# Threshold attention followed by a squared-ReLU feed-forward layer: one weight tile with fourteen stores, x^T loads in four periods, a reordered head with more unread transposes, and another order of the PSUM pools

## The chip, the cores and the metric

The kernel runs on one NeuronCore of a Trainium2 chip. The core has five engines that run side by side and meet at semaphores: TensorE (PE; its weight loads are listed as PEld), VectorE (DVE), ScalarE (ACT), GpSimd (POOL) and SyncE (SP), which here does nothing but issue DMAs. The metric is device time in microseconds; less is better. All data is float32, apart from the two weight matrices, which arrive as 64-bit floats and are converted on the chip.

## The reference

```
q, k, v: (8, 8, 576, 64)            # batch, heads, sequence, head size
scores = q @ k^T / 8
scores = where(scores >= rowmax(scores) - 0.02, scores, -1e9)
attn   = softmax(scores)             # divided by (sum + 1e-9)
x      = (attn @ v), heads side by side   # (4608, 512)
h      = maximum(x @ w_in, 0)             # w_in  (512, 2048)
out    = (h * h) @ w_out                  # w_out (2048, 512)
```

## The kernel before

**Attention.** The 64 heads are handled as 32 pairs. Queries come in blocks of 128 (four full ones per pair, and the remaining 64 rows of two pairs together), which gives 144 units; a unit covers both heads of its pair. The Python loop calls `period(p)` for p = -2 to 74, and a period takes two units, `A = 2p` and `B_ = 2p + 1`, through the stages of a software pipeline: scores, softmax, the transposes of the softmax weights of an earlier period (`fill`, `filled`), the product with v (`values`), and the store of the result to DRAM (`give_x`, then `ask`). The order in a period is written out by hand, and the engines keep it: each runs its own instructions strictly in the order in which they stand.

What matters for the change:

- `load_q`, `load_k`, `load_v` bring a pair's q, k, v. `turn(i, 0)` and `turn(i, 1)` transpose q and k of pair `i` on TensorE (four 128x128 transposes into the PSUM tile `pqk`), and ScalarE copies them out (lines 353 and 350). `turn_last` does the last 64 rows of both (`pqkr` or `pL`), with ScalarE copies in lines 369 and 370 and a GpSimd copy into the block-diagonal tile `kdiag` (line 373).
- `scores(n)` makes the 512 main columns of a unit's scores (line 411), `scores_rest(n)` the last 64 (line 386, which needs `kdiag`), into a PSUM tile `sc` of three banks. There are two such tiles, so unit n + 2 waits until VectorE has read unit n.
- VectorE takes the row maximum (`top`, line 428), ScalarE the exponential (line 436), VectorE masks and sums (line 441), GpSimd normalizes (line 453).
- `filled` copies transposed weights to SBUF on ScalarE (line 505). Its target `wT` exists once, and the results that `ask` stores to the DRAM tensors `xT` lie in the front of the same tile. So the copy of the next period waits for these stores to land.
- [...] During attention the pool `sc_pool` has two tiles of three banks and `b_pool` two tiles of one bank, which all other users take in turn.

**Weights, beside the attention.** `fetch` loads a chunk of w_out or w_in (line 183), `convert1` to `convert6` make 32-bit floats of it, one chunk per period, in the order of the periods: `convert1` stands in ScalarE's queue (line 203) ahead of the copies that end a `turn`. From period 15 on `sums` (GpSimd, lines 132 and 135) forms the 49 blocks of w_out that the fast matrix product needs, one or more per period. Since the blocks of w_in take the same places, `keep(m)` puts the seven finished blocks of row m on a list, and `ask(False)`, called twice in every period, stores up to two of them to DRAM each time (line 565). Stores, loads of q, k and v, weight chunks and results all stand in SP's one queue, in the order in which the periods issue them.

**Feed-forward.** Both products use 7-product block multiplication twice (49 products where 64 would be plain). Tokens go in nine steps of 512. `hidden_layer` (matmuls `ph`, line 807) makes squared hidden values and stores them to DRAM; in its last step `reload` brings the 49 blocks of w_out back (line 1028). `output_layer` (matmuls `po`, line 942) makes the output. `load_x(n)` loads a step's x^T with four or six DMAs (line 740). For step 0 that happens in period 27, at `IN_FIRST - 6`, and from period 34 on each period forms one of its block sums on GpSimd. The PSUM pool `banks` is opened when the attention's pools are closed: six tiles for products, and two tiles `c` for operands that `sum_v` copies through PSUM.

**The head.** Before the first period the kernel issues the loads of pair 0, ten transposes of the identity matrix whose result nobody reads (`keep_busy(10)`, line 996), then `turn(0, 0)`, `turn(0, 1)` and `turn_last(0)`. `TURNS` says in which period a later `turn` happens; those of g = 2 and g = 3 (q and k of pair 1) are both in period 1.

Of the kernel before, what the change touches and what calls it, by code (L numbers as in the profile page):

```python
# [10 lines left out]
FP32 = mybir.dt.float32  # L11
# [37 lines left out]
def kernel(  # L49
# [25 lines left out]
    nc = tc.nc  # L75
    B, H, S, D = q.shape
    P = 128
# [7 lines left out]
    BANK = 512  # L85
# [4 lines left out]

    PSUM = bass.MemoryType.PSUM
    const = ctx.enter_context(tc.tile_pool(name="const", bufs=1))
    wp = ctx.enter_context(tc.tile_pool(name="wp", bufs=1))
    dram = ctx.enter_context(tc.tile_pool(name="dram", bufs=1, space=bass.MemoryType.DRAM))
    xT = [dram.tile([DM, S], FP32, name=f"xT{b}") for b in range(B)]
    gT = [[dram.tile([P, BANK], FP32, name=f"g{n}_{j}") for j in range(16)] for n in range(NSTEP)]
# [9 lines left out]
    ident = const.tile([P, P], FP32, name="ident")  # L106
# [4 lines left out]
        out=tau_c[:, :], in_=bass.AP(tensor=tau.tensor, offset=tau.offset, ap=[[0, P], [1, 1]])  # L111
# [28 lines left out]
    OUTER, INNER = (1, 2, 6, 7, 4, 5, 3), (1, 6, 2, 7, 5, 4, 3)  # L140
# [5 lines left out]


    W_IN, W_OUT = {}, {}

    def weight_tile(W, m, k):  # L150
        at = OUTER.index(m) * 7 + INNER.index(k)
        W[m, k] = wp.tile([P, BANK], FP32, tag=f"w{at}", name="w")
        return W[m, k]

    def blocks(at):
# [101 lines left out]

    def keep(m):

        for k_ in INNER:  # L260
            w_dram[m, k_] = dram.tile([P, BANK], FP32, name=f"w{m}{k_}")
            later.append((w_dram[m, k_][:, :], W_OUT[m, k_][:, :]))

    later = deque()

# [199 lines left out]
    TURNS = {}  # L465
    for g in range(2, 2 * len(pairs)):
        two, x = divmod(g - 4, 4)
        TURNS.setdefault(max(1, (9 * two + 5 + 2 * x) // 2), []).append(g)

    def turned_last(p):  # L470

# [72 lines left out]
    def has(n):  # L544
        return 0 <= n < NU
# [12 lines left out]
    def ask(every=True):  # L558

        while given:  # L560
            to, from_ = given.popleft()
            nc.sync.dma_start(out=to, in_=from_)
        for _ in range(len(later) if every else min(2, len(later))):
            to, from_ = later.popleft()
            nc.sync.dma_start(out=to, in_=from_)

# [9 lines left out]
    def period(p):  # L576

        A, B_, a, b = 2 * p, 2 * p + 1, 2 * p - 2, 2 * p - 1
        m, turns = p - 2, TURNS.get(p, ())
        sc = {}  # L580

        def first(f, pv):
            if has(2 * m) or has(2 * m + 2):
                pt = pv[f] if pv else bank([P, BANK], "pX")
                fill(m + 1, f, pt)
                return pt

        def other(m, f):
            if has(2 * m):
                pt = bank([P, BANK], "pY")  # L590
                fill(m, f, pt)
                return pt

        def begin(n):
            if has(n) or has(n - 4):
                sc[n] = sc_pool.tile([P, 3 * BANK], FP32, tag="sc", name="sc")
            if has(n):
                scores_rest(n, sc[n])

        def spare(m, f, n):  # L600
            if has(2 * m):
                pt = sc[n][:, SPARE : SPARE + 3 * P]
                fill(m, f, pt)
                return pt

        pt3 = other(m, 4)
        then = None
        if turned_last(p):
            at = pt3 if pt3 else bank([P, BANK], "pL")
            then = turn_last(turns[-1] // 2, at[:, 3 * P : 4 * P])  # L610
        begin(A)
        do(b, "mask", 0)
        convert3(begun(p - 1))
        do(b, "mask", 1)
        ptA = spare(m, 2, A)
        if has(A):
            scores(A, sc[A])
            softmax(A, sc[A])
        if pt3:
            filled(m, 4, pt3)  # L620
        if then:
            then()
        last = [turn(g // 2, g % 2) for g in turns]
        if ptA is not None:
            aside(A, filled(m, 2, ptA))
        convert1(begun(p))
        pt2 = other(m, 3)
        do(a, "inverse")
        do(b, "over")
        do(A, "top")  # L630
        convert4(begun(p - 1))
        begin(B_)
        ptB = spare(m, 5, B_)
        do(a, "normal", 1)
        for done in last:
            done()
        if pt2:
            filled(m, 3, pt2)
        do(A, "least")
        if ptB is not None:  # L640
            aside(B_, filled(m, 5, ptB))
        do(A, "power", 0)
        do(a, "normal", 0)
        if has(B_):
            scores(B_, sc[B_])
            softmax(B_, sc[B_])
        do(b, "inverse")
        do(B_, "top")
        do(A, "power", 1)
        do(A, "mask", 0)  # L650
        do(A, "mask", 1)
        convert2(begun(p))
        pv = values(m) if has(2 * m) else None
        do(b, "normal", 1)
        do(B_, "least")
        pt0 = first(0, pv)
        pt1 = first(1, pv)
        do(b, "normal", 0)
        do(B_, "power", 0)
        sums_step()  # L660
        if pt0:
            filled(m + 1, 0, pt0, pv)
        convert5(begun(p - 1))
        do(A, "over")
        do(B_, "power", 1)
        if pt1:
            filled(m + 1, 1, pt1, pv)
        if pv:
            valued(m)
            give_x(m, wT[m + 1], plans[m + 1].size[0])  # L670
        ask(False)
        convert6(begun(p - 1))
        if begun(p - 1) is None:
            sums_step()
        sums_start(p)
        if begun(p - 1) is None and not turned_last(p):
            sums_step()
        fetch(begun(p + 2))
        ask(False)
        for n in (A, B_):  # L680
            if has(n) and units[n][1] == FULL:
                for i in units[n][0]:
                    turned.pop(i)
# [41 lines left out]

    prepared = {}

    def load_x(n):
        at = X_AT[n % 2]
        xo = arena[:, ds(at, 7 * BANK)].rearrange("p (m c t) -> p m c t", m=7, c=2)  # L730
        for a, c in ((0, 0), (1, 0), (1, 1), (0, 1)):
            to = xo[:, AT_B[a][c] - 1, :, :]

            t0 = n * STEP + c * 2 * NQ
            done = 0
            while done < 2 * NQ:
                b, at = divmod(t0 + done, S)
                m = min(S - at, 2 * NQ - done)
                src = xT[b][ds(a * 2 * P, 2 * P), ds(at, m)].rearrange("(c p) n -> p c n", p=P)
                nc.sync.dma_start(out=to[:, :, ds(done, m)], in_=src)  # L740
                done += m
        prepared[n] = (xo, None)

    def sum_v(op, out, x, y):

        c = banks.tile([P, BANK], FP32, tag="c", bufs=2, name="c")
        n = 1
        for m in y.shape[1:]:  # L750
            n *= m
        c = c[:, 0:n].rearrange("p (a b) -> p a b", b=y.shape[2])
        nc.scalar.copy(c, y)  # L753
        return lambda: op(nc.vector, out, x, c)
# [227 lines left out]
            w()  # L982

    with tc.manual_schedule():
        with ExitStack() as stack:
            sc_pool = stack.enter_context(tc.tile_pool(name="sc", bufs=2, space=PSUM))
            b_pool = stack.enter_context(tc.tile_pool(name="b", bufs=2, space=PSUM))

            def bank(shape, name):
                return b_pool.tile(shape, FP32, tag="b", name=name)  # L990

            def keep_busy(times):

                pt = bank([P, P], "idle")
                for _ in range(times):
                    nc.tensor.transpose(pt[:, :], ident[:, :], ident[:, :])

            load_q(0)
            load_k(0)
            first = sb.tile([P, 4, 2], FP32, tag="small", bufs=4, name="small")  # L1000
            nc.scalar.activation(out=first[:, 0, :], in_=ident[:, 0:2], func=AF.Exp)
            load_v(0)
            keep_busy(10)
            turn(0, 0)()
            turn(0, 1)()
            turn_last(0, bank([P, P], "pqkr")[:, :])()
            for i in range(1, 3):
                load_v(i)
            xsums = iter(())
            for p in range(-2, NU // 2 + 3):  # L1010
                period(p)
                if p == IN_FIRST - 6:
                    load_x(0)
                    xsums = prepare_x(0, lambda op, out, x, y: op(nc.gpsimd, out, x, y))
                if p > IN_FIRST:
                    next(xsums, None)
            for _ in xsums:
                pass
            for _ in range(60):
                sums_step()  # L1020
            ask()
        banks = ctx.enter_context(tc.tile_pool(name="banks", bufs=1, space=PSUM))

        def reload(at):

            m, k = OUTER[at // 7], INNER[at % 7]
            t = weight_tile(W_OUT, m, k)
            nc.sync.dma_start(out=t[:, :], in_=w_dram[m, k][:, :])

        for n in range(NSTEP):  # L1030
            last = n == NSTEP - 1
# [103 lines left out]
```

## Time and profile before

| | us |
|---|---|
| median of 3 runs | 1383.01 |
| lowest and highest run | 1382.67, 1388.16 |
| the profiled execution | 1383.25 |
| its span on the engines | 1381.5 |
| TensorE busy | 1339.5 (97%) |
| VectorE, GpSimd, ScalarE busy | 1025.5, 990.1, 860.5 |
| DMA traffic | 177.24 MB |

In the rows of the timeline the first number is the start in us from the start of the span, the second the duration, then the engine, the line, the operation, and its tiles (output first) with shapes and count; brackets at the end give how long the engine was idle before it and what ended that. SPq is SP's issue of a DMA: its duration is that of the issue, and not of the transfer. In the tables by stage each pair of numbers is busy us and instructions of PE, PEld, DVE, ACT and POOL; the last three columns are the granted TensorE clock, the mean busy share of the DMA engines, and GB/s. The attention lasts to about 583 us of the span, the hidden layer to 981, the output layer to the end. A matmul of 128x128 float32 operands is two instructions in the trace.

### The profile page before, as it was taken

To read this page: it belongs to the slowest core of one execution; us is meant where nothing else is said; L and a number is where in the kernel's file an instruction comes from. 1 tells how busy PE (TensorE), PEld (TensorE's weight loads), DVE (VectorE), ACT (ScalarE), POOL (GpSimd) and SP (SyncE) were. 2 spreads that over 40 slices of the span, in tenths; PEclk is the share of its full clock that TensorE was granted. 3 is DMA by queue.
4 is the path that set the end of the run, shared out by engine and by line. 5 is a ranking of instruction groups with operands and counts; after the bars stand their busy time and mean duration, and the time that the engine had idled before them with its cause. 6 is when DMAs were issued, how large, how long until landed. Compare 5 with 4: busy or idle time off the path is not lost. (4 is left out here: it accounts for less than half of the span.)

```text
span 1381.5 us, 40859 instructions
## 1 busy us (share of the span) xinstructions
PE 1339.5 (97%) x15882; PEld 1180.6 (85%) x15882; DVE 1025.5 (74%) x2136; ACT 860.5 (62%) x1651; POOL 990.1 (72%) x1111
## 2 busy tenths in 40 slices
PE   7999999899999999999999999999999999999998
PEld 4676767666767676799999999999999999999998
DVE  5999988789998888577778777887666456654563
ACT  5999877789987777656766566765733224332330
POOL 2777888798888886355566556656877777777776
PEclk9999999999999999999999999999999999999999
DMA  4554325786532322123432343338962344224411
GB/s 115 128 150 127 92 63 149 222 260 192 139 89 67 73 65 57 36 83 129 146 128 87 108 146 130 108 106 325 370 223 64 120 154 153 93 71 144 153 32 31
DMA packets 205295, 177.24 MB, mean 128 GB/s; under 512 B 96304, under 2 KB 149552, under 8 KB 205104
## 3 DMA queue, kind: packets, MB, share of 16 engines
q1 hardware_dynamic: 203792, 174.24, 40.9%
q8 instruction: 125, 2.05, 0.6%
q14 instruction: 66, 0.54, 0.1%
q10 hardware_dynamic: 1312, 0.41, 0.1%
HBM read 105.12 MB, written 69.47 MB: 126 GB/s over the span
## 5 line engine op out<-in xcount | busy, mean ns | idle before, releaser
L135 POOL TENSOR_TENSOR arena<-arena 128x512 f32<-128x512 f32 (+1 forms) x314 | 376.4, 1221 | 250.1 <-DVE arena L135 210.4
L807 PE MATMUL ph<-arena,w 128*128 128x128 f32 x3528 | 396.6, 275 | 1.8 <-ACT arena L505 0.8
L807 PEld LDWEIGHTS ph<-arena,w 128*128 128x128 f32 x3528 | 394.7, 192 | 3.7 <-DVE arena L135 2.8
L942 PE MATMUL po<-w,arena 128*128 128x128 f32 x3528 | 396.6, 275 | 0.3
L942 PEld LDWEIGHTS po<-w,arena 128*128 128x128 f32 x3528 | 394.8, 192 | 1.9 <-issue 1.6
L135 DVE TENSOR_TENSOR arena<-ph,arena 128x512 f32<-128x512 f32 x378 | 255.3, 688 | 93.7 <-PE ph L807 62.4
L441 DVE SCALAR_TENSOR_TENSOR arena<-sc,arena 128x576 f32<-128x576 f32 x288 | 223.0, 811 | 16.4 <-ACT arena L436 16.0
L428 DVE TENSOR_REDUCE arena<-sc 128x2 f32<-128x1152 f32 x144 | 195.1, 1355 | 53.5 <-PE sc L411 49.2
L135 DVE TENSOR_TENSOR arena<-po,arena 128x128 f32<-128x128 f32 x378 | 107.8, 289 | 169.7 <-PE po L942 166.2
L436 ACT ACTIVATE arena<-sc,arena 128x576 f32<-128x576 f32 x288 | 207.2, 750 | 42.3 <-DVE arena L428 36.7
L453 POOL TENSOR_SCALAR arena<-arena 128x576 f32<-128x576 f32 x288 | 213.9, 757 | 19.0 <-DVE arena L450 11.2
L753 ACT COPY c<-arena 128x512 f32<-128x512 f32 (+1 forms) x303 | 172.8, 580 | 62.4 <-DVE arena L132 55.0
L516 PEld LDWEIGHTS pv<-arena 64*64 64x64 f32 x5760 | 151.6, 133 | 40.1 <-issue 21.7
L132 POOL TENSOR_TENSOR arena<-arena 128x512 f32<-128x512 f32 (+1 forms) x138 | 174.5, 1264 | 9.7
L132 DVE TENSOR_TENSOR arena<-arena,c 128x512 f32<-128x512 f32 (+1 forms) x267 | 174.5, 661 | 7.5 <-ACT c L753 6.5
L411 PE MATMUL sc<-arena 64*64 64x512 f32 x1152 | 159.5, 624 | 0.0
L516 PE MATMUL pv<-arena 64*64 64x128 f32 (+1 forms) x5760 | 157.9, 259 | 0.4 <-ACT arena L353 0.2
L786 ACT ACTIVATE arena<-arena 128x512 f32<-128x512 f32 x144 | 89.9, 624 | 76.9 <-POOL arena L135 76.7
L721 ACT COPY arena<-po 128x128 f32<-128x128 f32 x63 | 16.6, 264 | 179.2 <-PE po L942 177.4
L499 PE MATMUL pY<-ident,arena 128*128 128x128 f32 x546 | 85.9, 278 | 28.3 <-ACT arena L505 24.8
L447 POOL TENSOR_SCALAR arena<-arena 128x2 f32<-128x2 f32 x144 | 47.5, 330 | 83.9 <-DVE arena L441 46.1
L499 PEld LDWEIGHTS pY<-ident,arena 128*128 128x128 f32 x546 | 60.0, 140 | 51.9 <-issue 25.3
(63 smaller groups left out, 1247.6 us busy)
## 6 DMA issues: line engine op xcount, KB each, us to landing
g<-arena SPq DMA_DIRECT2D x144, 256.0 KB, 2.0
arena<-g SPq DMA_DIRECT2D x144, 256.0 KB, 4.6
w<-w SPq DMA_DIRECT2D x98, 256.0 KB, 5.1
arena<-in_v_dram SPq DMA_DIRECT2D x32, 288.0 KB, 3.1
out_dram<-arena SPq DMA_DIRECT2D x70, 128.0 KB, 2.2
arena<-in_q_dram SPq DMA_DIRECT2D x64, 128.0 KB, 3.2
arena<-in_moe_w_out_dram SPq DMA_DIRECT2D x16, 512.0 KB, 4.3
xT<-arena SPq DMA_DIRECT2D x128, 64.0 KB, 2.1
```

Of the source, the lines that this page charges most:

```text
L132: e.tensor_tensor(out=out, in0=x, in1=y, op=ALU.subtract)
L135: e.tensor_tensor(out=out, in0=x, in1=y, op=ALU.add)
L411: made = nc.tensor.matmul(sc[at, ds(j * 2 * BANK, MAIN)], lhs, kT[rows, 0:MAIN], start=True, stop=True)
L428: nc.vector.tensor_reduce(out=nmx, in_=both, axis=AXIS.X, op=ALU.max, negate=True)
L436: nc.scalar.activation(out=w[:, :, j, :], in_=of(j), func=AF.Exp, bias=nmx[:, j : j + 1], scale=1.0)
L441: nc.vector.scalar_tensor_tensor(out=w[:, :, j, :], in0=of(j), scalar=thr[:, j : j + 1], in1=w[:, :, j, :], op0=ALU.is_ge, op1=ALU.mult, a ...
L453: nc.gpsimd.tensor_scalar(out=w[:, :, j, :], in0=w[:, :, j, :], scalar1=rs[:, j : j + 1], scalar2=1.0, op0=ALU.mult, op1=ALU.mult)
L499: nc.tensor.transpose(to, w[:, c, :, :].rearrange("p j d -> p (j d)"), ident[:, :])
L516: nc.tensor.matmul(out[j][ds(u * D, D), ds(row, count)], loaded_v[i][rows, c, :], x[rows, ds(plans[m].at[u, c] + row, count)], start=(c == ...
L753: nc.scalar.copy(c, y)
L807: nc.tensor.matmul(to[:, j, :], W_IN[m, k][:, ts(j, P)], of[k][:, m - 1, :], start=(not more and j == 0), stop=True, skip_group_check=True,)
L942: nc.tensor.matmul(to, g[:, j, :], w[:, j, :], start=(not more and j == 0), stop=(j == 3), skip_group_check=True)
```

## The change

It has five parts.

1. The 49 separate weight tiles become slices of one tile `wall`. `keep(m)` makes one DRAM tensor of seven blocks per row m and lists two stores in place of seven, one of four blocks (128x2048) and one of three (128x1536): 14 stores in all. `ask(False)` sends at most one store, and its second call in a period is gone. `reload` reads slices of the new DRAM tensors.
2. The four loads of x^T for step 0 go out one per period, in periods 23 to 26.
3. The head has more unread TensorE work: 15 transposes in place of 10; between `turn(0, 0)` and `turn(0, 1)` eight 64-row transposes, two whole ones, sixteen 64x64 matmuls and two whole ones again; four after `turn_last(0)`; twenty after period 0.
4. In period 0 the main scores of unit 0 stand ahead of its last 64 columns, and the `turn` of pair 1's q moves from period 1 to period 0.
5. `b_pool` is opened first and stays open to the end; the feed-forward's pool `banks` then has the six product tiles alone, and `sum_v` takes its tiles from `b_pool`.

```diff
-        W[m, k] = wp.tile([P, BANK], FP32, tag=f"w{at}", name="w")
+        W[m, k] = wall[:, ds(at * BANK, BANK)]
...
-        for k_ in INNER:
-            w_dram[m, k_] = dram.tile([P, BANK], FP32, name=f"w{m}{k_}")
-            later.append((w_dram[m, k_][:, :], W_OUT[m, k_][:, :]))
+        to = dram.tile([P, 7 * BANK], FP32, name=f"w{m}")
+        for i, k_ in enumerate(INNER):
+            w_dram[m, k_] = to[:, ts(i, BANK)]
+        for i, z in ((0, 4), (4, 7)):
+            at = OUTER.index(m) * 7 + i
+            later.append((to[:, ds(i * BANK, (z - i) * BANK)], wall[:, ds(at * BANK, (z - i) * BANK)]))
...
-        TURNS.setdefault(max(1, (9 * two + 5 + 2 * x) // 2), []).append(g)
+        TURNS.setdefault(max(g - 2 if g < 4 else 1, (9 * two + 5 + 2 * x) // 2), []).append(g)
...
-        for _ in range(len(later) if every else min(2, len(later))):
+        for _ in range(len(later) if every else min(1, len(later))):
...
-            if has(n):
+            if n > 0 and has(n):
                 scores_rest(n, sc[n])
...
             scores(A, sc[A])
+            if A == 0:
+                scores_rest(A, sc[A])
             softmax(A, sc[A])
...
         fetch(begun(p + 2))
-        ask(False)
...
-        c = banks.tile([P, BANK], FP32, tag="c", bufs=2, name="c")
+        c = b_pool.tile([P, BANK], FP32, tag="b", name="c")
...
     with tc.manual_schedule():
+        b_pool = ctx.enter_context(tc.tile_pool(name="b", bufs=2, space=PSUM))
         with ExitStack() as stack:
             sc_pool = stack.enter_context(tc.tile_pool(name="sc", bufs=2, space=PSUM))
-            b_pool = stack.enter_context(tc.tile_pool(name="b", bufs=2, space=PSUM))
...
+            def keep_halves(times):
+                pts = [bank([P, BANK], "idle") for _ in range(2)]
+                for i in range(times):
+                    for r in range(2):
+                        rows = ds(r * HALF, HALF)
+                        nc.tensor.transpose(pts[r][:, ts(i, HALF)], ident[rows, :], ident[rows, rows])
+
+            def keep_quarters(times):
+                pts = [bank([P, BANK], "idle") for _ in range(2)]
+                for i in range(times):
+                    for r in range(2):
+                        rows = ds(r * HALF, HALF)
+                        for c in range(2):
+                            nc.tensor.matmul(
+                                pts[r][ds(c * HALF, HALF), ts(i, HALF)], ident[rows, ds(c * HALF, HALF)],
+                                ident[rows, rows], start=True, stop=True,
+                            )
...
-            keep_busy(10)
+            keep_busy(15)
             turn(0, 0)()
+            keep_halves(4)
+            keep_busy(2)
+            keep_quarters(4)
+            keep_busy(2)
             turn(0, 1)()
             turn_last(0, bank([P, P], "pqkr")[:, :])()
+            keep_busy(4)
...
                 period(p)
+                if p == 0:
+                    keep_busy(20)
+                if IN_FIRST - 10 <= p < IN_FIRST - 6:
+                    load_x(0, XPARTS[p - IN_FIRST + 10 :][:1])
                 if p == IN_FIRST - 6:
-                    load_x(0)
                     xsums = prepare_x(0, lambda op, out, x, y: op(nc.gpsimd, out, x, y))
```

## The prediction

> **What bounds the kernel now.** I read the page first, then the busy time by stage, then the timeline of the places where a stage is not at its own pace.
>
> ```profile
> PE 1339.5 (97%) x15882; PEld 1180.6 (85%) x15882; DVE 1025.5 (74%) x2136; ACT 860.5 (62%) x1651; POOL 990.1 (72%) x1111
> ...
> PE 29%; DVE 0%; issue 0%; DVEq 0%
> ...
> 0.00:18.00 18.00, 11.12 (x42) 5.93 (x42) 5.26 (x11) 6.12 (x12) 2.54 (x15) 1.00 0.55 144
> ...
> 221.58:237.24 15.66, 15.01 (x269) 10.87 (x265) 12.73 (x29) 12.13 (x24) 13.42 (x19) 1.00 0.68 207
> 237.24:252.90 15.66, 12.84 (x216) 9.46 (x212) 10.77 (x24) 10.00 (x20) 11.97 (x17) 1.00 0.77 228
> ...
> 583.00:1378.00 795.00, 793.03 (x7056) 789.47 (x7056) 529.16 (x1062) 389.02 (x736) 536.09 (x440) 1.00 0.40 135
> ```
>
> TensorE bounds everything. From 583 us on it lacks 2 us in 795, and the change takes no matmul out of that. So the gain can only lie in TensorE's idle time before 583. An undisturbed period is 7.83 us (15.66 for two), with 15.01 of 15.66 busy. The change does not touch the small waits inside it. What is left are four places: the head (6.9 us idle in 18), the two periods from 237 to 253 (2.2 us less matmul time than their neighbours), the three periods from 278 to 304 (below), and the joint at 583.
>
> The starts of VectorE's row maxima (line 428) give the periods. Their distances are 7.3 to 7.9 us nearly throughout; the exceptions are 8.36 (period 0), 10.26 (period 29, from 237.62), and 8.75, 8.60 and 8.48 (periods 34 to 36, from 278.50).
>
> **The head.**
>
> ```profile
> 1.45 2.40 PE L996 MATMUL idle<-ident 128*128 128x128 f32 x10 [1.45 <-POOL ident masks.py:199]
> ...
> 4.73 1.09 PE L345 MATMUL pqk<-ident,arena 128*128 128x128 f32 x4 [0.89 <-DMA arena<-in_q_dram]
> ...
> 5.85 0.69 ACT L353 ACTIVATE arena<-pqk,qscale 128x512 f32<-128x512 f32 x1 [0.88 <-PE pqk L345]
> ...
> 6.27 1.09 PE L345 MATMUL pqk<-ident,arena 128*128 128x128 f32 x4 [0.46 <-DMA arena<-in_k_dram]
> ...
> 9.74 1.99 PE L411 MATMUL sc<-arena 64*64 64x512 f32 x8
> ...
> 11.80 1.36 DVE L428 TENSOR_REDUCE arena<-sc 128x2 f32<-128x1152 f32 x1 [7.87 <-PE sc L411]
> ...
> 17.41 0.77 PE L386 MATMUL sc<-arena 128*128 128x128 f32 x2 [2.64 <-DVE arena L431]
> ...
> 20.03 1.95 PE L345 MATMUL pqk<-ident,arena 128*128 128x128 f32 x8
> ...
> 22.13 1.09 PE L411 MATMUL sc<-arena 64*64 64x512 f32 x8
> ...
> 27.94 0.66 PE L345 MATMUL pqk<-ident,arena 128*128 128x128 f32 x4
> ```
>
> The same eight score matmuls take 1.99 us at 9.74 and 1.09 at 22.13, four transposes 1.09 and then 0.66: TensorE runs at about half speed until some 21.8 us, although the granted clock reads 1.00 in every row, so that column does not show it. The change fills TensorE's gaps with unread work and takes pair 1's transposes out of the chain. Worked out in order:
>
> - Fifteen transposes at (2.40 - 0.43)/9 = 0.22 us end near 4.9, about when q is there. Cost nothing; q's landing at 4.73 hides them, to within 0.2 us.
> - The half transposes write two PSUM tiles, and the second is the one from which ScalarE still copies q (line 353, to 6.54). So TensorE waits until 6.6, and k's transposes, which could start at 6.27, are queued behind all fillers: seven half transposes of 0.11, four whole ones of 0.22, sixteen 64x64 matmuls at 0.06 (the value product's 72 instructions of twice the columns take 2.15 us warm, so 0.03 a matmul warm): 2.6 us cold, 1.4 warm. k's transposes start at 9.2 or 8.1. ScalarE, GpSimd's `kdiag` copy and SP's loads of pair 1's k, which wait for these transposes, all wait with them; those loads then land near 16, and pair 1 is first needed later.
> - From there, warm: transposes 0.66, copy 0.6, four unread transposes 0.5, scores 1.09 and latencies 0.3, last columns 0.3, so the first row maximum is 3.4 after: 11.5. Before it is at 11.80. If the switch comes only near 11: 9.2 + 1.09 + 0.6 + 0.5 + 1.4 = 12.9.
> - From unit 0's row maximum to unit 4's (28.14) it is 16.34 us before. Warm, with one `turn` between: unit 1 follows after 2.2 (2.64 before); then VectorE's chain (two maxima of 1.36, four masks of 0.81, small ones) puts unit 2 at 6.9 (8.36 before), unit 3 at 9.0, and unit 4, by the measured 4.85 from 23.29 to 28.14, at 13.85. That is 2.5 us less. The twenty transposes after period 0 (2.2 us warm) lie in the wait for VectorE's masks (2.6 us idle before 17.41); without that cover they would cost their 2.2.
>
> When is TensorE warm? The Trainium skill ("TensorE: Matmul & The Clock Gate", Part 1: The HAM clock gate) says that about 3.4 us of sustained work, in a free-running window, opens the clock, typically about 4 us in. This trace does not simply agree: from 9.02 to 14.77 TensorE has no gap, 5.75 us, mostly score matmuls on quarters of the array, and 17.41 is still slow (0.77 for what takes 0.42 at 21.79). But 4.4 us from 17.41 to 21.8, half of them whole transposes, end with the switch. The new stretch from 1.45 to 5.82 is also 4.4 us, whole transposes throughout. By the rule it opens at 5.5, and the head gains 2.5 + 0.3 = 2.8; by the long row it opens only with the next stretch, near 11, and the gain is 2.5 - 1.1 = 1.4. The nearest row is just at the edge, so I take **-2.1 us**. Ends: -3.4 (k's transposes at 7.5), and +0.5 (cold to 15, row maximum at 14.2, then 14.1).
>
> **Period 29.**
>
> ```profile
> 229.81 2.85 SPq L565 DMA_DIRECT2D w<-w  x3
> 232.71 2.23 SPq L740 DMA_DIRECT2D arena<-xT  x4
> ...
> 241.55 1.91 SPq L562 DMA_DIRECT2D xT<-arena  x3
> ...
> 244.92 0.48 ACT L505 COPY arena<-pv 128x384 f32<-128x384 f32 x1 [2.52 <-DMA xT<-arena]
> ```
>
> ScalarE's copy into `wT` waits 2.52 us for result stores, which SP issues at 241.55, five us behind their usual place (one period after 228.54 is 236.4), since three weight stores, four x^T loads and eight loads stand ahead. After the change one weight store of some 0.5 us and no x^T load stand there (they cost 0.4 to 0.6 each in periods 23 to 26, whose SP queue has several us free). k and v then go out by 236.8, the results at 236.9, and they land near 241, before the copy wants them at 242.4. The period falls from 10.26 to 7.83: **-2.4 us**. If the stores are late by another way, 0.
>
> **Periods 34 to 36.**
>
> ```profile
> ACT arena L203 <- DMA arena<-in_moe_w_in_dram: 3.8, 5, 1.8
> ...
> 279.80 0.69 ACT L203 ACTIVATE arena<-arena 128x512 f32<-128x512 f32 x1 [1.79 <-DMA arena<-in_moe_w_in_dram]
> ```
>
> Period 34 loses 0.92 to a weight chunk that lands late. But GpSimd works from 276.5 to 317 with one wait over 0.1 us before 309 (0.35 at 284.89), at 8.5 us a period, and its instructions stay as they are. So I credit **-0.35**; ends -2.3 (0.92, 0.77 and 0.65, all three periods back to 7.83) and a loss, for which see the last rival.
>
> **The joint at 583.**
>
> ```profile
> 582.46 0.62 ACT L505 COPY arena<-pv 128x128 f32<-128x128 f32 x2 [2.07 <-PE pv L516]
> ...
> 583.14 22.04 PE L807 MATMUL ph<-arena,w 128*128 128x128 f32 x195 [0.75 <-ACT arena L505]
> ```
>
> The first hidden matmuls wait 0.75 us for ScalarE's last copies out of `b_pool`. With `b_pool` kept apart, the changed program, as built, makes them wait for TensorE alone. ScalarE is free again for the first hidden copy in time (it needs the product 1.2 us later). Nothing follows but dense matmul: **-0.75**, ends 0 and -0.9.
>
> **At nothing.** One tile or 49: the same addresses are ordered, engines other than SP and TensorE issue the same list but for the moved q copy. Reloads come in the same 256 KB pieces, ten steps of 0.9 us ahead and 5.1 us to landing. `sum_v` has two PSUM tiles as before. Fewer stores save SP 35 issues of 0.46 us, which are on the path in period 29 alone; the bytes are the same.
>
> **Sum.** -2.1 - 2.4 - 0.35 - 0.75 = -5.6 against the profiled 1383.25 (span 1381.5), which is 0.24 above the median: 1377.65, or **1377.4** as a median. That is 0.4%. What a measurement of this kernel can tell from no change is about 0.5%, 6.9 us, so the likeliest result is just inside it.
>
> **The rivals.**
>
> - *Everything at its good end*, 1374.7: head -3.4, period 29 -2.4, periods 34 to 36 three quarters of their 2.3, joint -0.75: -8.3. For it: the new work covers TensorE without a gap from the start, and those three periods follow a late chunk. Against: GpSimd has no slack there.
> - *The clock does not open early*, 1379.5: head 0. For it: 5.75 us without a gap did not open it before. Then 2.6 us of fillers ahead of k buy nothing but the later periods' return.
> - *The large stores hold up the weight chunks*, slower, 1394. In periods 31 to 38 `fetch` now stands behind one store of up to 1.05 MB, not two of 0.26. The Trainium skill ("DMA: Bandwidth & Descriptors", Queues, rings and completion order) says that each DMA engine takes its descriptors in ring order; the page's best slice moves 370 GB/s, so 0.52 MB more is 1.4 us later, with the DMA busy share there already at 1.0. Chunks now land in 3.8 to 6.1 us, and `convert1` waits in ScalarE's queue with the copies of q and k behind it, which TensorE's next transposes and scores need. A wait of 1.79 cost 0.92, so 3.2 would cost 2.3, seven times 16, less the other 5.2: +11. It turns the sign when seven periods lose 0.75 each, a wait of 1.6 in each. By the rule alone it happens. Against it by the trace: the chunk's issue moves 0.5 to 1 us earlier in SP's queue, since one store issue in place of two is ahead, only one of the waits exceeded 0.8, and the bytes per period are the same, so I put the net at 0.
>
> **How the numbers follow.** The forecast's case has 0.5 (its own range 1375.3 to 1379.7, from the head's two ends and the joint), the good end 0.3, the late clock 0.14, the held-up chunks 0.06. The limits of 0.5% are 1376.1 and 1389.9. Faster by more: 0.3 and a fifth of the forecast's case, 0.4. Slower: 0.06. Within: 0.54. The range is 1373.5 to 1382: a us below the good end, up to the late clock with period 29 half cured, and it leaves out the last rival.
>
> **What would show it.** Right: scores at 1.1 us instead of 1.99 in the first unit or the second, unit 4's row maximum near 26.0 in place of 28.14; no wait of ScalarE on xT in period 29; hidden matmuls following the last value product within 0.2 us. Wrong: line 203 waiting over 1.5 us in several periods; the first row maximum after 14; result stores issued late in any period from 23 to 39; a hidden layer longer than 397 us.

## The result, and the profile after

The changed kernel takes 1378.53 us in the median (1376.37 to 1381.16), against 1386.55 for the kernel before in the same comparison: ratio 0.9948, interval 0.9929 to 0.9968. In a second comparison of the same program, with more executions, the ratio is 0.9966 (0.9954 to 0.9978; 1380.24 against 1384.51). So two sets of one program can differ by 1.7 us in the median. The forecast, 5.6 us of 1383.25, is 0.996. The median of before in the table above, 1383.01, came from three executions; larger sets give 1384.5 to 1385.2, and single ones lie between 1382 and 1389.

The profiled execution of the changed kernel took 1381.16 us (span 1379.4), only 2.1 us less than the one of before. Where those 2.1 us are can be read from the starts of the row maxima (line 431 now). Lead over before: 0.29 us at unit 4, 0.24 at period 29, 2.07 at period 30, 2.49 at period 37, 1.05 at period 70, 2.1 at the end. So in this execution the head gave almost nothing, period 29 gave 1.8, periods 34 to 36 gave 0.4, periods 39 and 56 took 1.4 back, and the joint gave 1.05.

First the page and the busy time by stage of the changed kernel; the columns are those of before:

```profile
PE 1342.9 (97%) x15955; PEld 1185.5 (86%) x15955; DVE 1026.6 (74%) x2136; ACT 861.2 (62%) x1651; POOL 991.7 (72%) x1111
...
0.00:18.00 18.00, 15.06 (x118) 11.31 (x119) 4.77 (x10) 6.77 (x13) 2.11 (x14) 1.00 0.43 100
...
237.38:253.65 16.27, 15.03 (x233) 10.87 (x233) 12.60 (x29) 12.19 (x24) 13.60 (x21) 1.00 0.68 205
...
581.00:1376.00 795.00, 793.32 (x7073) 789.68 (x7064) 529.15 (x1061) 389.53 (x737) 536.74 (x440) 1.00 0.40 135
```

TensorE is busy for 15.06 of the first 18 us, not 11.12, and yet VectorE did less there (4.77 us, before 5.26): the added work is unread, and it did not bring the softmax forward. The dense part is unchanged.

The head of the changed kernel, from its timeline:

```profile
4.75 1.09 PE L348 MATMUL pqk<-ident,arena 128*128 128x128 f32 x4
...
6.61 0.69 PE L1009 MATMUL idle<-ident 64*128 64x64 f32 x7 [0.48 <-ACT arena L356]
...
7.88 1.25 PE L1017 MATMUL idle<-ident 64*64 64x64 f32 x32
...
9.55 0.91 PE L348 MATMUL pqk<-ident,arena 128*128 128x128 f32 x4
...
11.72 1.09 PE L414 MATMUL sc<-arena 64*64 64x512 f32 x8
...
13.27 1.36 DVE L431 TENSOR_REDUCE arena<-sc 128x2 f32<-128x1152 f32 x1 [9.38 <-PE sc L389]
...
23.98 1.09 PE L502 MATMUL pY<-ident,arena 128*128 128x128 f32 x4 [1.70 <-ACT arena L508]
...
26.06 1.65 PE L414 MATMUL sc<-arena 64*64 64x512 f32 x8
...
27.85 1.36 DVE L431 TENSOR_REDUCE arena<-sc 128x2 f32<-128x1152 f32 x1 [1.60 <-PE sc L414]
```

The fillers behind ScalarE's copy (line 356) hold k's transposes back to 9.55; before they stood at 6.27. TensorE's clock opened (went from half to full speed) near 10: 0.91 is between 1.09 and 0.66, and the scores at 11.72 are fast. The row maximum of unit 0 came at 13.27 (before 11.80), and then the clock closed again: four transposes take 1.09 at 23.98 and the scores 1.65 at 26.06. Unit 4 is at 27.85, where it was at 28.14.

The closing stands in the column of the granted clock, once the stretches are cut where the trace's clock record changes. The slow time ahead of the first opening does not: that record begins at 10.18 with the opening, and the column reads 1.00 for what lies before.

```profile
0.00:10.18 10.18, 8.25 (x66) 6.92 (x67) 0.21 (x2) 2.17 (x3) 1.63 (x11) 1.00 0.49 113
...
20.42:23.83 3.41, 1.44 (x12) 0.42 (x4) 3.38 (x7) 2.43 (x6) 2.62 (x4) 1.00 0.61 174
23.83:27.25 3.42, 3.27 (x17) 2.09 (x17) 2.32 (x8) 2.65 (x6) 1.10 (x3) 0.50 0.51 146
```

Period 29 and the joint:

```profile
237.58 1.91 SPq L565 DMA_DIRECT2D xT<-arena  x3
...
242.85 0.48 ACT L508 COPY arena<-pv 128x384 f32<-128x384 f32 x1 [0.67 <-DMA xT<-arena]
...
319.20 0.69 ACT L203 ACTIVATE arena<-arena 128x512 f32<-128x512 f32 x1 [1.87 <-DMA arena<-in_moe_w_in_dram]
...
581.28 2.94 PE L813 MATMUL ph<-arena,wall 128*128 128x128 f32 x24
581.43 0.63 ACT L508 COPY arena<-pv 128x128 f32<-128x128 f32 x2 [2.06 <-PE pv L519]
```

The result stores are issued at 237.58 where they were issued at 241.55; the copy waits 0.67 us for them, not 2.52, and the period takes 8.43 us, not 10.26. That is still not the undisturbed 7.83. A weight chunk is waited for in period 39, which takes 9.08 us. The first hidden matmul starts ahead of ScalarE's last copies, with no idle time in front.

### The profile page after: what moved, and what is told of

Read it like the earlier page. It is cut to its first block, busy times and chain, and to the rows that moved or that the text cites. A ratio compares the mean times of both kernels' runs of the same rounds, so it can differ in the third digit from the quotient of the medians.

```text
span 1379.4 us, 40958 instructions
## 1 busy us (share of the span) xinstructions
PE 1342.9 (97%) x15955; PEld 1185.5 (86%) x15955; DVE 1026.6 (74%) x2136; ACT 861.2 (62%) x1651; POOL 991.7 (72%) x1111
## 4 chain that ended last, share of the span: by engine, by line
PE 54%; DVE 2%; POOL 1%; ACT 1%; issue 1%; DMA 0%; DVEq 0%; POOLq 0%; SPq 0%; ACTq 0%
PE po L948 29%; PE ph L813 25%; DVE arena L134 2%; POOL arena L134 1%; ACT arena L792 0%; ACT arena L725 0%; PE pv L519 0%; DMA wall<-w 0%; POOL arena L456 0%; ACT arena L508 0%; PE pY L502 0%; DVE arena L131 0%; DVEq L134 0%; ACT arena L793 0%; POOLq L134 0%
## 5 line engine op out<-in xcount | busy, mean ns | idle before, releaser
L813 PE MATMUL ph<-arena,wall 128*128 128x128 f32 x3528 | 396.6, 275 | 1.1 <-DVE arena L134 0.5
L813 PEld LDWEIGHTS ph<-arena,wall 128*128 128x128 f32 x3528 | 394.7, 192 | 2.9 <-DVE arena L134 2.8
L948 PE MATMUL po<-wall,arena 128*128 128x128 f32 x3528 | 396.6, 275 | 0.3
L948 PEld LDWEIGHTS po<-wall,arena 128*128 128x128 f32 x3528 | 394.8, 192 | 2.0 <-issue 1.6
L456 POOL TENSOR_SCALAR arena<-arena 128x576 f32<-128x576 f32 x288 | 214.7, 760 | 19.4 <-DVE arena L453 11.5
```

Of the source, the lines that this page charges most:

```text
L456: nc.gpsimd.tensor_scalar(out=w[:, :, j, :], in0=w[:, :, j, :], scalar1=rs[:, j : j + 1], scalar2=1.0, op0=ALU.mult, op1=ALU.mult)
L813: nc.tensor.matmul(to[:, j, :], W_IN[m, k][:, ts(j, P)], of[k][:, m - 1, :], start=(not more and j == 0), stop=True, skip_group_check=True,)
L948: nc.tensor.matmul(to, g[:, j, :], w[:, j, :], start=(not more and j == 0), stop=(j == 3), skip_group_check=True)
```

## The experiments

Ratios are to the kernel before, with their 95% intervals, from executions that alternate with it on the same chip.

### The parts alone

`head_only` is the kernel before with parts 3 and 4 of the diff above:

> The kernel before with parts 3 and 4 alone (unread work, order of unit 0, early turn of pair 1's q). Theory of the sum as predicted: 2.1 us faster, and period 29 still long (10.3 us), hidden matmuls still waiting for ScalarE. Rival, 'the head steadies the clock': the timed executions of the kernel before lie at 1383 or at 1386 to 1388, since its clock opens at different moments; then this part alone brings 4 to 5 us in the median and its runs lie within 2 us of each other. Second rival, 'the large gain is the queue': 0 to 0.5 us here, as between the two profiled executions (unit 4's row maximum 0.3 us earlier).

1383.78 us, ratio 0.9993 (0.9983 to 1.0003), scatter 1379.7 to 1387. In its profile the clock opened early and the head gave 3.5 us, more than the 2.1 forecast, and then period 29 took 2.2 of it back. Timeline of `head_only`, and two stretches of its period 29:

```profile
4.84 0.63 PE L345 MATMUL pqk<-ident,arena 128*128 128x128 f32 x4
...
8.15 0.60 PE L345 MATMUL pqk<-ident,arena 128*128 128x128 f32 x4
...
11.55 1.36 DVE L428 TENSOR_REDUCE arena<-sc 128x2 f32<-128x1152 f32 x1 [7.53 <-PE sc L386]
...
24.67 1.36 DVE L428 TENSOR_REDUCE arena<-sc 128x2 f32<-128x1152 f32 x1
...
242.35 0.48 ACT L505 COPY arena<-pv 128x384 f32<-128x384 f32 x1 [3.42 <-DMA xT<-arena]
...
242.98 0.52 PE L499 MATMUL pY<-ident,arena 128*128 128x128 f32 x3 [3.71 <-ACT arena L505]
...
244.51 1.99 PE L411 MATMUL sc<-arena 64*64 64x512 f32 x8
```

```profile
240.17:243.58 3.41, 0.60 (x6) 0.63 (x7) 0.07 (x1) 1.23 (x3) 2.31 (x2) 1.00 0.79 274
243.58:246.99 3.41, 3.41 (x17) 1.47 (x16) 1.93 (x6) 1.55 (x5) 2.03 (x5) 0.50 0.93 247
```

Unit 4 is 3.5 us earlier than before (24.67 against 28.14). In period 29 ScalarE waits 3.42 us for the result stores, TensorE stands idle for 3.71 and comes back slow: the scores at 244.51 take 1.99 us. The period takes 12.48 us. So the late transfer is paid twice here, once as idle time and once as a closed clock (granted 0.50 from 243.58 to 246.99). In the profile of before, where TensorE was busy for 1.56 us of the emptiest such stretch of period 29, the clock stayed open.

`dma_only` has parts 1 and 2 alone, `stores_only` part 1 (as in the diff above, with `load_x(0)` left in period 27), `xload_only` part 2:

```diff
+                if IN_FIRST - 10 <= p < IN_FIRST - 6:
+                    load_x(0, XPARTS[p - IN_FIRST + 10 :][:1])
                 if p == IN_FIRST - 6:
-                    load_x(0)
```

> The kernel before with parts 1 and 2 alone (14 stores, x^T loads over four periods). Sum as predicted: 2.75 us faster, period 29 near 7.9 us, periods 34 to 36 a little shorter. 'The head steadies the clock': 1 to 2 us faster and the executions scatter over 5 us as before. 'The gain is the queue': 5 us or more.

> The kernel before with part 1 alone (one weight tile, 14 stores, one store call a period; the four x^T loads stay together in period 27). Parts 1 and 2 together gave 0.9975. Period 29 was late because three weight stores, four x^T loads and eight loads stood ahead of the result stores. Theory 'the x^T loads are the surplus': period 29 stays over 9 us and the gain is under 1.2 us. Theory 'the stores are': period 29 falls to about 8.5 and the gain is 2.5 us or more.

> The kernel before with part 2 alone (the four x^T loads one a period in periods 23 to 26; 49 stores as before). 'The x^T loads are the surplus': period 29 falls below 8.5 us and the gain is 2 us or more. 'The stores are': period 29 stays over 9 us, gain under 1 us.

| | median, us | ratio | period 29, us |
|---|---|---|---|
| dma_only | 1381.06 | 0.9975 (0.9968 to 0.9981) | 7.83 |
| stores_only | 1384.39 | 0.9993 (0.9985 to 1.0002) | 9.81 |
| xload_only | 1382.18 | 0.9975 (0.9963 to 0.9987) | 7.83 |

Part 2 alone brings all of it; part 1 alone brings nothing that can be measured. SP's issues in `stores_only`, then ScalarE's copy in it, and the same in `xload_only`, where no wait stands:

```profile
229.44 1.50 SPq L568 DMA_DIRECT2D w<-wall  x1
230.98 2.63 SPq L742 DMA_DIRECT2D arena<-xT  x4
...
240.49 1.91 SPq L565 DMA_DIRECT2D xT<-arena  x3
...
244.08 0.48 ACT L508 COPY arena<-pv 128x384 f32<-128x384 f32 x1 [2.06 <-DMA xT<-arena]
```

```profile
231.64 2.69 SPq L565 DMA_DIRECT2D w<-w  x3
...
240.61 1.92 SPq L562 DMA_DIRECT2D xT<-arena  x3
...
244.32 0.48 ACT L505 COPY arena<-pv 128x384 f32<-128x384 f32 x1
```

The four x^T loads cost SP 2.63 us and stay; one store instead of three saves 1.35. With the x^T loads gone, three stores do no harm in this profile. In the five profiles with the four loads in one place (before, `head_only`, `before_again`, `joint_only`, `stores_only`) period 29 takes 9.45 to 12.48 us; in the profiles with the loads spread it takes 7.83 to 8.45. `dma_only` also scatters less: 1380.3 to 1383.6, where the kernel before lies between 1381.9 and 1388.0 in the same comparison. `xload_only` was profiled in an execution whose clock opened at 12.8 and closed again from 16.2 to 23.0 and from 26.5 to 29.9, with period 1 at 10.32 us; its time there, 1383.45, is above its median.

`joint_only` has part 5 alone:

```diff
-        c = banks.tile([P, BANK], FP32, tag="c", bufs=2, name="c")
+        c = b_pool.tile([P, BANK], FP32, tag="b", name="c")
...
+        b_pool = ctx.enter_context(tc.tile_pool(name="b", bufs=2, space=PSUM))
```

> The kernel before with part 5 alone (b_pool kept open, product tiles in the other pool). Sum as predicted: 0.75 us faster; the pair of profiles says 1.05. The first hidden matmul follows the last value product at once, and ScalarE's last copies run beside it. Rivals: 0, if something else was as late as those copies, and in that case an idle time of 0.5 us or more stands ahead of line 807 or in the first products.

1383.95 us, ratio 0.9995 (0.9984 to 1.0006): by the times alone not to be told from nothing. The timeline resolves it:

```profile
583.41 3.84 PE L807 MATMUL ph<-arena,w 128*128 128x128 f32 x32
583.55 0.62 ACT L505 COPY arena<-pv 128x128 f32<-128x128 f32 x2 [2.06 <-PE pv L516]
```

No idle time stands ahead of line 807. From the row maximum that starts period 70 to the end of the span it is 820.2 to 820.6 us in the eight profiles of kernels with part 5, and 821.1 to 821.5 in the six of kernels without it. So part 5 is worth about 1.0 us in the profiled executions (0.9 between `joint_only` and before).

`before_again` (the kernel before, a comment added):

> The kernel before once more, with a comment added. It measures what no change looks like: ratio 1.000 with an interval of about 0.002 either way. If its profiled execution is one of the long ones (1386 to 1388), the comparison with the profile shown shows where those 4 to 5 us are: by 'the head steadies the clock' all of them before unit 8's row maximum at 43.8 us; by 'the queue' in period 29 and periods 34 to 40.

Ratio 1.0001 (0.9993 to 1.0008). Its profile was a short execution (1382.41), so it does not show where the long ones lose their time. It shows the scatter of the late transfers, though: period 29 at 9.45 us, period 34 at 9.34, against 10.26 and 8.75.

### What the head is worth, and what in it

`after_again` is the changed kernel with a comment added; `after_old_head` takes parts 3 and 4 back:

```diff
-            keep_busy(15)
+            keep_busy(10)
             turn(0, 0)()
-            keep_halves(4)
-            keep_busy(2)
-            keep_quarters(4)
-            keep_busy(2)
...
-            keep_busy(4)
...
-                if p == 0:
-                    keep_busy(20)
```

and the same for the order of unit 0 and for `TURNS`.

> The changed kernel once more, beside its own variants. Parts alone gave -0.0025 (queue), -0.0007 (head) and -0.0005 (pools), -0.0037 in sum; the first comparison gave -0.0052. Theory 'the head's gain was eaten in period 29 when the queue was not mended' (TensorE idle there for 3.9 us, then cold): the whole is more than its parts, 0.9945 to 0.9955. Rival 'the parts add': 0.996 to 0.9965. Of the clock: its first scores may come warm or cold from execution to execution, and the runs scatter by 3 to 5 us; if the clock opens by 5.5 us, unit 4's row maximum is near 24.7, if near 10, at 27.9.

> The changed kernel with the head of before (parts 3 and 4 undone; queue and pools changed). Against the changed kernel it tells what the head is worth once period 29 is mended. As predicted (head 2.1 us): 1380 when the changed kernel is at 1378. 'The head's gain was eaten in period 29': 2 to 3 us slower than the changed kernel. 'The head brings nothing' (0.3 us between the two profiles first shown): the same within 0.7 us. Its runs scatter less than those of the kernel before (2 to 3 us).

1380.24 us, 0.9966 (0.9954 to 0.9978), and 1380.36 us, 0.9967 (0.9954 to 0.9979). With period 29 mended, the new head as a whole shows no gain in the median (0.1 us), though intervals of 1.7 us to either side leave room for most of the 2.1 forecast. Its executions scatter more widely (1376.1 to 1383.2, against 1379.5 to 1381.7). The idea that the gain had been eaten in period 29 explains the profile of `head_only`; as the explanation of the median it finds no support. The timeline of `after_again` has the late clock and the second closing too:

```profile
24.53 1.08 PE L502 MATMUL pY<-ident,arena 128*128 128x128 f32 x4 [1.70 <-ACT arena L508]
...
26.62 1.73 PE L414 MATMUL sc<-arena 64*64 64x512 f32 x8
```

Unit 4 is at 28.49 there, and at 28.43 with the old head.

`after_no_gap_fill` is the changed kernel without the fillers ahead of k:

```diff
             turn(0, 0)()
-            keep_halves(4)
-            keep_busy(2)
-            keep_quarters(4)
-            keep_busy(2)
             turn(0, 1)()
```

> The changed kernel without the unread work between the transposes of q and k of pair 0 (halves, quarters and the two pairs of whole ones); the 15, 4 and 20 unread transposes and the order of unit 0 stay. k's transposes can then start at 6.3 instead of 8.2 to 9.5. Theory of the prediction: the fillers cost 1.5 to 2.6 us here and are paid back by an open clock, so without them the row maximum of unit 0 comes 1 to 1.5 us earlier when the clock has opened by 5.5, and later when it has not; in the median 0 to 1 us slower or faster, with more scatter. Rival 'the fillers only delay': 1 to 2.5 us faster in every run. Rival 'they hold the clock open': 2 us or more slower.

1376.58 us (1374.96 to 1379.22), ratio 0.9946 (0.9933 to 0.9960): 3.7 us below the changed kernel by the medians of this set. The size is not settled: the intervals of the two ratios overlap, and the changed kernel's first set had 0.9948. "The fillers only delay" is the nearest of the three, but not in every run: two of the six executions took 1379.1 and 1379.2. Timeline:

```profile
5.12 0.63 PE L348 MATMUL pqk<-ident,arena 128*128 128x128 f32 x4 [0.21 <-DMA arena<-in_q_dram]
...
6.46 0.63 PE L348 MATMUL pqk<-ident,arena 128*128 128x128 f32 x4 [0.71 <-DMA arena<-in_k_dram]
...
8.35 1.09 PE L414 MATMUL sc<-arena 64*64 64x512 f32 x8
...
9.90 1.36 DVE L431 TENSOR_REDUCE arena<-sc 128x2 f32<-128x1152 f32 x1 [6.11 <-PE sc L389]
...
23.25 1.36 DVE L431 TENSOR_REDUCE arena<-sc 128x2 f32<-128x1152 f32 x1
```

Here the clock was open by 5.00 us, after the fifteen transposes, k's transposes come as soon as k is there, and unit 4 is at 23.25, 4.9 us before the kernel of before.

`after_fetch_first`, in which the store follows the fetch:

```diff
-        ask(False)
+        ask(None)
...
         fetch(begun(p + 2))
+        store_one()
...
-        for _ in range(len(later) if every else min(1, len(later))):
+        for _ in range(len(later) if every else 0):
...
+    def store_one():
+        if later:
+            to, from_ = later.popleft()
+            nc.sync.dma_start(out=to, in_=from_)
```

> The changed kernel with the weight store put behind the fetch of the next weight chunk in each period, not ahead of it. In the changed kernel one chunk was waited for 1.87 us (period 39 took 9.08 us). Theory 'the store holds up the chunk': the chunks land in 3 to 4 us instead of 5.2, ScalarE's waits on them (1.9 to 3.5 us in the profiles) go, and it is 1 to 2 us faster. Rival 'the DMA engines are full there anyway, or GpSimd sets the pace': within 0.5 us of the changed kernel, and q, k or results are late instead.

1378.55 us, ratio 0.9958 (0.9945 to 0.9971), 0.6 us of waiting for chunks in its profile, w_in chunks landing after 4.3 us, not 5.2. Against 0.9966 (0.9954 to 0.9978) that is not told apart.

`best` has both edits, and `best_hold` beside them:

```diff
+        if p == 1:
+            keep_busy(12)
         pt0 = first(0, pv)
```

> The changed kernel without the unread work between the first two turns and with the fetch of a weight chunk ahead of the store. Alone they gave 0.9946 and 0.9958 where the changed kernel gave 0.9966. If the two gains are in different places they add: 0.993 to 0.994, 1375 us. If the second was chance (5 executions): as the first alone, 1376.6.

> The kernel 'best' with twelve more unread transposes in period 1, ahead of the first transposes of the softmax weights, where TensorE stood idle for 2 us of 3 and the clock closed again in the changed kernel's profile (four transposes 1.09 us at 23.98, eight score matmuls 1.65 at 26.06). Theory 'the clock closes there in a part of the executions': the slow executions become fewer, the median is 0.5 to 1 us lower and the scatter smaller. Rival 'that was one execution, the early clock matters alone': no difference within 0.5 us; if the transposes push back real work, 0.5 us slower.

`best`: 1374.70 us (1374.46 to 1376.04), ratio 0.9921 (0.9909 to 0.9933), the fastest kernel here; in its profile no wait for a chunk or for result stores is left on ScalarE in the attention. `best_hold`: 1375.67 us, 0.9928 (0.9916 to 0.9940), not told apart. The timeline of `best` shows what the fillers are good for:

```profile
6.55 0.63 PE L348 MATMUL pqk<-ident,arena 128*128 128x128 f32 x4 [0.73 <-DMA arena<-in_k_dram]
...
7.86 0.98 PE L1008 MATMUL idle<-ident 128*128 128x128 f32 x4 [0.40 <-ACT arena L353]
8.77 1.99 PE L414 MATMUL sc<-arena 64*64 64x512 f32 x8
...
24.69 1.36 DVE L431 TENSOR_REDUCE arena<-sc 128x2 f32<-128x1152 f32 x1
```

Without them the clock, open since 4.62, closed again at 8.03, and the first scores took 1.99 us. Even so unit 4 was at 24.69, where `head_only`, with its fillers and the clock open from 4.64 on, had it at 24.67: a closed clock costs 0.9 us in one score product, and the fillers put k's transposes 1.6 to 3.9 us later (8.15 to 9.97 in the profiles with them, 6.10 to 6.55 without).

The head's profiles side by side, with the changes from the clock record of each trace (us from the start):

| profile | fillers ahead of k | clock opens | closes again | first row maximum | unit 4 |
|---|---|---|---|---|---|
| changed kernel | yes | 10.18 | 23.83 to 27.25 | 13.27 | 27.85 |
| `after_again` | yes | 10.89 | 24.54 to 27.96 | 13.84 | 28.49 |
| `after_fetch_first` | yes | 6.34 | 23.41 to 26.82 | 11.87 | 26.18 |
| `head_only` | yes | 4.64 | not in the head | 11.55 | 24.67 |
| `best` | no | 4.62 | 8.03 to 11.45 | 11.52 | 24.69 |
| `after_no_gap_fill` | no | 5.00 | no | 9.90 | 23.25 |
| `best_hold` | no | 6.13 | no | 9.54 | 23.05 |
| before (old head) | no | 21.84 | no | 11.80 | 28.14 |

With the clock open early and kept open, the fillers cost 1.4 to 1.6 us at unit 4 (24.67 against 23.25 and 23.05, one profile each). How often each kernel's clock opens early, and so what the fillers cost in a median, the profiles do not say.

## Why the prediction was right, and where it was not

The sum came out: 1378.53 for 1377.4, and 0.4% forecast for 0.52% (first comparison) and 0.34% (second). That is in part luck, since the terms did not all come out: the head's 2.1 us do not show in the median, while the x^T loads gave 3.5 us in the times for 2.4 forecast, and the joint 1.0 in the profiles for 0.75.

- **The head, -2.1: not borne out.** Measured: 0.1 us by the medians of `after_again` and `after_old_head`, 1.1 by those of `head_only` and the kernel before; the intervals do not exclude 2.1, but in the two profiles of the changed kernel unit 4 is 0.3 us earlier and 0.35 later than before. Its first steps hold. k's transposes were put at 8.1 or 9.2; they came at 8.15 (`head_only`) and 9.55. The first row maximum was put at 11.5 or 12.9; it came at 11.55 and 13.27. What failed is the step "from there, warm ... unit 4 at 13.85". Where the clock opens by 5 and stays open it is 13.1 to 13.4 after unit 0; in the changed kernel it is 14.6, since TensorE works for only 1.44 us between 20.42 and 23.83 and the clock closes again. The prediction priced the opening of the clock and not its closing.
- **When TensorE is warm: asked of the wrong quantity.** The prediction compared the lengths of stretches without a gap. In the traces the clock changes only at whole multiples of 3.41 us from its first change. Counted back from the opening at 21.84, the 5.75 us without a gap in the kernel before are cut at 11.60 into 2.58 and 3.17 us of work, while the stretch from 18.42 to 21.84 is full. The new work of 4.4 us fills such a stretch in `head_only` (3.20 us of it from 1.23 to 4.64) and falls across a cut at 3.35 in the changed kernel (1.90 and 2.93). So "early or late" was a matter of where the cuts fell; the value midway was a guess, and both profiles of the changed kernel have the late case.
- **Period 29, -2.4: right in place and near in size**, 1.8 in the changed kernel's profile, and 2.4 in the six profiles of other kernels with both edits, where the period takes 7.83. The times of `xload_only` give 0.25% (3.5 us, from 1.8 to 5.1). Part 1 had no share in it that can be measured: it is the x^T loads.
- **Periods 34 to 36, -0.35: right.** They take 25.83 us together before and 25.41 after; the profiles of `stores_only` and `xload_only` have 25.87 and 25.89, that of `dma_only` 25.35, so it seems to need both (`joint_only`, with neither, has 25.61). That GpSimd sets their pace fits the small gain, and was not tested.
- **The joint, -0.75: right**, about 1.0; the matmuls now start even a little ahead of the last value product's modelled end.
- **At nothing: right** for the one tile and for the reloads: `stores_only`, which has both, is at 0.9993.
- **The rival of the held-up chunks** is there at most in small: w_in chunks take 5.2 us to land in place of 4.5, and one wait of 1.87 us stands in period 39, which is 1.25 us longer than an undisturbed one. That the large stores caused this wait is not shown: `joint_only`, with the small stores and 4.4 us to landing, has waits of 1.62 and 1.51 nearby, and `after_again` has none over 0.5.
- **The rival "the clock does not open early"** is what the changed kernel's two profiled executions did, at 1381.16 and 1380.24. A median near the good end, 1374.7, was reached only by kernels without the fillers ahead of k.
- **Its own signs.** Fast scores in the first unit and no gap ahead of the hidden matmuls came; unit 4 near 26.0 and period 29 without a wait on xT did not (27.85, and 0.67 us). The forecast's own range is also off: its ends for the head (-3.4, +0.5) and the joint (-0.9, 0) give about 1376.0 to 1380.8, not 1375.3 to 1379.7.

The longest executions of the kernel before (1386 to 1388) go with a clock that closed again. None was profiled, but the mean granted clock of every timed execution is on record. Of 105 executions of before in the three later sets, 34 took 1386 us or more, and 30 of these have 0.997 or less; of the 71 shorter ones 12 have. The 26 at 0.995 average 1387.2 us, the 63 at 0.998 or more 1384.1. A mean of 0.995 is about 14 us at half clock. In `dma_only` no execution is below 0.996. Where in the kernel those 14 us lie stays open. An estimate from two profiles: three closed stretches in the head put unit 4 at 29.92 in `xload_only`, 1.8 us late, and one in period 29 made that 2.2 us longer in `head_only`; 1383.25 and these 4.0 are 1387.3.

## What to carry to other kernels

Unread work that keeps TensorE's clock open must stand where TensorE would wait anyway, and never ahead of the operand that the chain needs next: here, with the clock open in either case, the fillers ahead of k put unit 4 1.4 to 1.6 us later, and an open clock at the first scores is worth 0.9. In a queue that issues everything in one order, look for the burst, not for the number of transfers: four loads spread over four periods were worth all that 35 fewer stores were not. Price an idle gap of TensorE as the gap and, where it leaves less than about half of a 3.41 us stretch busy, as 3.41 us of slow matmuls after it.

## What the runs showed of the hardware

- TensorE runs at full or at half clock, by its recent work. In the 14 profiles the changes lie on a grid of 3.41 us, and each of the nine closed stretches between the first opening and the end of the matmuls lasts 3.41 or 6.83 us. The granted clock shows these as 0.50, but reads 1.00 for the slow time ahead of the first opening, which only the durations show.
- The grid does not start with the kernel. The same work from 1.45 to 5.82 us, without a gap, opened the clock at 4.64 in `head_only` and not before 10.18 in the changed kernel. That agrees with the Trainium skill ("TensorE: Matmul & The Clock Gate", Part 1: The HAM clock gate), which has a window of 3.4 us that runs freely and does not start with the kernel. The skill has the opening after some 4 us of work; here 4.4 us were enough in some executions only.
- Ahead of all 14 first openings TensorE was busy for 3.08 us or more of a stretch (by its modelled ends), and no stretch of 2.94 or less was followed by one. Three of 3.17 to 3.22, mostly score matmuls on quarters of the array, were not either.
- The clock also closes in the middle of work. During the attention all eight open stretches with 1.49 us of work or less were followed by a closing (0.60 us from 240.17 in `head_only`, 1.44 from 20.42 in the changed kernel); of those with 1.56 to 2.18 us one was (1.93, in `best`) and twelve were not.
- A store of 1 MB was issued in 0.6 us in the changed kernel (at 229.58) and landed after 5.2 in the median; four stores of 256 KB took SP 2.1 us to issue in the kernel before (at 243.50). Alone, in `stores_only`, that difference bought nothing that can be measured (0.9993).
